# Two extra 512-column products ahead of each head's weight transposes, in the first eight heads of a fused attention and MLP kernel

## The chip, the core and the metric

The kernel runs on one core of a Trainium2 chip. The time is the device time of one execution in microseconds. The core has TensorE (matmuls, PE in the profile, with its weight loads as PEld), VectorE (DVE), ScalarE (ACT), GpSimd (POOL) and SyncE (SP, which issues nearly all DMAs). The engines run side by side, each takes its own instructions in a fixed order, and they wait for each other by semaphores. TensorE's clock is granted at one of two levels, 1.2 and 2.4 GHz; the profile shows it as a share of the higher one.

## What is computed

A causal attention with decay over 4 batches of 8 heads, 576 positions and 64 dimensions, and after it two MLP layers without bias, 512 to 2048 to 512, over the 2304 tokens:

```python
scores = scale * np.matmul(q, k.transpose(0, 1, 3, 2))
cum = np.cumsum(np.log(np.clip(f, 0.0001, 1.0)), axis=-1)
scores = np.where(causal, -1e9, scores + cum[:, :, :, None] - cum[:, :, None, :])
attn = np.exp(scores - np.max(scores, axis=-1, keepdims=True))
attn = attn / (np.sum(attn, axis=-1, keepdims=True) + 1e-09)
x = np.matmul(attn, v)                       # then heads side by side: (2304, 512)
h = x @ w_in;  x = (h - np.tanh(h)) @ w_out  # first layer
h = x @ w2_in; r = np.maximum(h, 0.0); out = (r * r) @ w2_out
```

## The kernel before

The attention is cut into 64 units: 32 for the first 256 queries of every head (`n` below 32) and 32 for the other 320. The first eight units are the eight heads of batch 0. They are worked alone, as two heads at a time, since the first layer can only start when a block of 256 tokens has all its heads; the loop over `astream[:n_start]` near the end of `fused_kernel` does so, with a higher priority (`HOT`). From there on the first layer's products and the other attention units are merged by a table of due times. The order that each engine gets is in the end set by a scheduler: it takes what is ready by its own estimate of times, so that an instruction that is added in one place can change the order around it on all engines.

For a pair of heads TensorE does: four transposes of q and k (`tkq`, line 397, copied to `XF` by VectorE, line 398), the scores (`s`, line 512), the transposes of the softmaxed weights `Pb` (`pt`, in `pt_atom`, lines 539 to 572), copied by ScalarE to `PTF` (line 553), the products with v (`pv`, line 596), scaled by VectorE to `xq` (line 605), and their transposes (`xt`, line 611), which ScalarE and VectorE split into the high and the low part of `x` (lines 663, 664). GpSimd makes the decay (lines 361 and 365), VectorE takes it and the maximum (line 474), and ScalarE the exponential (line 483).

`keep_warm(m)` (line 1000) puts `m` products of 128 by 128 with 512 columns on TensorE. They multiply a tile of ones and write into a bank of PSUM, `warm_out`, that nothing reads (line 1003). Each is held behind what was written on TensorE before it (`keep_in_program_order`); nothing else orders it. Before the change it is called once, ahead of the transposes of unit 0, with `WARM` = 8. The tile `warm` is one of three buffers of a ring `g`, which the first layer's tanh uses later, and `warm_out` is the bank `y1`, which the first layer's sums (`y`, line 819) use later.

The weights come as 64-bit packed words and are decoded while the attention runs: for each of 16 chunks of a layer, `load_w` (line 140) issues two loads of 512 KB, one for either half, on SyncE's queue. `decode_w` takes each half through two conversions on ScalarE (lines 154, 155) and two bit operations on VectorE (lines 161, 163), and then splits each half into a high part (ScalarE, line 176) and a low part (line 177: GpSimd for the first half, VectorE for the second). The first layer multiplies with chunk after chunk: `h` (line 779) needs the chunk's w_in, tanh is taken by ScalarE (line 789), VectorE subtracts it (line 792), ScalarE and VectorE split the difference (796, 800), and `y` (line 819) multiplies it with the chunk's w_out. Every fp32 value is split in two parts of fewer bits so that three fast products replace a slow one. In this text weight 3 is chunk 3 of the first layer, `w_0_3` in the code's names.

Of the kernel before, what the change touches and what calls it, by code (L numbers as in the profile page):

```python
# [18 lines left out]
B, H, S, D = 4, 8, 576, 64  # L19
# [27 lines left out]
WARM = 8  # L47
# [57 lines left out]
def fused_kernel(ctx: ExitStack, tc: tile.TileContext, q, k, v, f, w1i, w1o, w2i, w2o, out):  # L105
# [14 lines left out]
    def bank(tag, n, name):  # L120
        return ps.tile([P, 512], F32, tag=tag, name=name, bufs=n)
# [417 lines left out]
    def pt_atom(i):  # L539

        n, ts = slots[i]
        pb = Pb[i % RING]

        def a():
            while i not in ready_p:
                cw.step()
            if i == 0:
                keep_warm(WARM)
            t = bank("a", 4, f"pt_{i}")
            if len(ts) > 1:  # L550
                for x, (o, c) in enumerate(((0, 0), (128, 0), (128, 1))):
                    nc.tensor.transpose(t[:, x * P : x * P + P], pb[:, o + c * P : o + c * P + P], ident)
                cw.later(LAG['tr'], lambda: nc.scalar.activation(ptf(n), t[:, 0 : 3 * P], AF.Copy))
                return
            if not PT:
                for x in range(2):
                    PT.append(ap.tile([P, 1344], F32R, tag=f"PT{x}", name=f"PT{x}", bufs=1))
                    nc.gpsimd.memset(PT[x][:, 128:192].bitcast(F32), 0.0)
            ti, rows, o, w = ts[0]
            nch = ti + 1  # L560
            for x in range(nch):
                s0 = o + (nch - 1 - x) * P

                nc.tensor.transpose(t[:, x * rows : x * rows + P], pb[:, s0 : s0 + P], ident)  # L564
            src = t[:, 0 : nch * rows].rearrange("p (c r) -> p c r", c=nch)
            dst = [strided(PT[x], *PTC[ti], nch, rows) for x in range(2)]

            def ev():
                nc.scalar.activation(dst[0], src, AF.Copy)  # L569
                cw.later(LAG['trlo'], lambda: nc.vector.tensor_tensor(dst[1], src, dst[0].bitcast(F32), op=ALU.subtract))  # L570
            cw.later(LAG['tr'], ev)
        return 2 * sum((ti + 1) * rows for ti, rows, _, _ in ts), a

    def strided(t, d0, step, m, rows):
        x = t[:, d0 : d0 + rows]
        return bass.AP(tensor=x.tensor, offset=x.offset, ap=[x.ap[0], [step, m], [1, rows]])
# [4 lines left out]
    def ptf(n):  # L581

        return PTF[n % 6 // 3][:, n % 3 * 384 : n % 3 * 384 + 384]
# [416 lines left out]
    def keep_warm(m):  # L1000

        for _ in range(m):
            tc.keep_in_program_order(nc.tensor.matmul(warm_out, lhsT=warm[:, :P], rhs=warm, start=True, stop=True))
# [50 lines left out]
    for s in range(len(steps) + behind):  # L1054
        if s < len(steps):
            i, fc = steps[s]
# [45 lines left out]
```

## Time and profile before

| | |
|---|---|
| Median of 3 runs | 1066.9 us (1065.85 to 1067.23) |
| The profiled execution, its own time | 1066.61 us |
| its span | 1064.9 us |
| mean granted clock | 0.989 |
| TensorE busy | 98% of the span |
| VectorE, ScalarE, GpSimd busy | 56%, 51%, 28% |

A busy share is a mean over stages with different limits. The stages here are: the sums of logs and the first scores (0 to some 20 us), the eight heads (to 41.4 us), block 0 of the first layer merged with further heads while the weights are being decoded (to some 139 us), and then the two layers to the end, with the rest of the attention merged in. Matmuls are pipelined and the profile models their ends, so a product counts as busy for longer than it holds up the next: the distance from one start to the next tells its price. A row of a timeline gives the start, the length, the engine, the line, the operation with what it writes and reads, the count, and in brackets how long the engine stood idle before it and what ended that.

### The profile page before, as it was taken

Reading aid. Unit: us, or ns where it says so; the run is one execution under the profiler, and the core shown is the slowest. Engines: PE = TensorE matmul, PEld = TensorE weight load, DVE = VectorE, ACT = ScalarE, POOL = GpSimd, SP = SyncE. Lnnn points to the kernel's source line nnn. Section 1 sums busy time; section 2 is a strip of 40 time slices with the busy share of each in tenths; the row PEclk is TensorE's granted clock in tenths of the full one; section 3 lists DMA queues with packets and bytes.
Section 4 is the critical chain, followed back from the end, with each engine's and each line's share of the span. In section 5 each row is a group of like instructions: output and inputs, shape, how many; then the busy total and the mean of one; then the engine's idle time right before and its main releaser. Section 6 shows DMA issues by size and latency. Waiting matters only on the chain.

```text
span 1064.9 us, 18194 instructions
## 1 busy us (share of the span) xinstructions
PE 1041.0 (98%) x6545; PEld 934.7 (88%) x6545; DVE 596.3 (56%) x1397; ACT 544.5 (51%) x1179; POOL 293.0 (28%) x468
## 2 busy tenths in 40 slices
PE   7989999999999999999999999999999999999998
PEld 5778899999999999999999887888888888888887
DVE  4897863577777776777854688822322322332332
ACT  5886764566656666666743677622322322222232
POOL 5455532355555555654520121100000000000000
PEclk9998899999999999999999999999999999999999
DMA  8776552242243342433203555300200200010010
GB/s 218 240 214 174 175 150 69 68 125 73 69 128 79 99 118 70 108 98 81 75 21 117 178 189 187 119 1 0 80 1 1 79 1 1 20 40 1 1 40 20
DMA packets 126970, 93.87 MB, mean 88 GB/s; under 512 B 79552, under 2 KB 112128, under 8 KB 126880
## 3 DMA queue, kind: packets, MB, share of 16 engines
q1 hardware_dynamic: 126832, 92.68, 30.1%
q8 instruction: 52, 0.85, 0.3%
q14 instruction: 38, 0.31, 0.1%
q10 hardware_dynamic: 48, 0.03, 0.0%
HBM read 74.26 MB, written 13.71 MB: 83 GB/s over the span
## 4 chain that ended last, share of the span: by engine, by line
PE 79%; DVE 5%; issue 3%; ACT 2%; DMA 1%; POOL 1%; DVEq 0%; ACTq 0%; POOLq 0%
PE h L939 19%; PE o L981 18%; PE h L779 14%; PE y L819 14%; PE pt L564 4%; PE pv L635 3%; PE s L526 2%; PE s L527 2%; DVE wfull L163 2%; PE pv L596 1%; DVE wraw L161 1%; DVE ghl L800 1%; ACT ghl L796 1%; DMA K<-K 1%; POOL w L177 1%
## 5 line engine op out<-in xcount | busy, mean ns | idle before, releaser
L819 PE MATMUL y<-ghl,w 128*128 128x256 f32 (+1 forms) x1536 | 245.2, 303 | 0.1
L819 PEld LDWEIGHTS y<-ghl,w 128*128 128x128 f32 x1536 | 211.3, 192 | 11.7 <-DVE ghl L800 1.9
L779 PE MATMUL h<-x,w 128*128 128x256 f32 x1344 | 205.1, 293 | 9.4 <-POOL w L177 7.5
L939 PE MATMUL h<-y,w 128*128 128x512 f32 (+1 forms) x960 | 209.9, 368 | 0.0
L981 PE MATMUL o<-w,ghl 128*128 128x512 f32 x864 | 209.0, 389 | 0.0
L939 PEld LDWEIGHTS h<-y,w 128*128 128x128 f32 x960 | 169.3, 188 | 31.3
L779 PEld LDWEIGHTS h<-x,w 128*128 128x128 f32 x1344 | 177.1, 192 | 17.2 <-POOL w L177 10.3
L981 PEld LDWEIGHTS o<-w,ghl 128*128 128x128 f32 x864 | 161.1, 188 | 32.7
L952 DVE TENSOR_TENSOR r<-r 128x512 f32<-128x512 f32 (+1 forms) x80 | 51.9, 648 | 216.3 <-ACT r L949 216.3
L949 ACT ACTIVATE r<-h 128x512 f32<-128x512 f32 (+1 forms) x80 | 44.4, 555 | 219.9 <-PE h L939 219.9
L483 ACT ACTIVATE Pb<-Pb,st 128x384 f32<-128x384 f32 (+2 forms) x96 | 67.6, 705 | 69.8 <-DVE st L474 69.7
L369 POOL TENSOR_SCALAR Pb<-neg,ccol 128x384 f32<-128x384 f32 (+2 forms) x96 | 69.2, 721 | 92.2 <-PE pt L564 74.8
L497 POOL TENSOR_SCALAR Pb<-Pb,st 128x384 f32<-128x384 f32 (+2 forms) x96 | 66.0, 688 | 82.5 <-DVE st L493 48.2
L177 POOL TENSOR_TENSOR w<-wfull,w 128x512 fp32r<-128x512 f32 x32 | 43.0, 1342 | 156.9 <-ACT w L176 156.8
L474 DVE CUSTOM_DVE_ANT_0 Pb<-s,Pb 64x288 f32<-64x288 f32 (+2 forms) x160 | 74.0, 476 | 16.4 <-PE s L527 7.7
L957 DVE TENSOR_TENSOR ghl<-r,ghl 128x512 fp32r<-128x512 f32 (+1 forms) x80 | 51.0, 638 | 44.7 <-ACT ghl L953 41.4
L953 ACT ACTIVATE ghl<-r 128x512 fp32r<-128x512 f32 (+1 forms) x80 | 47.1, 588 | 51.5 <-DVE r L952 51.5
L792 DVE TENSOR_TENSOR g<-h,g 128x512 f32<-128x512 f32 x72 | 49.4, 687 | 35.9 <-ACT g L789 34.6
L800 DVE TENSOR_TENSOR ghl<-g,ghl 128x512 fp32r<-128x512 f32 x72 | 55.6, 772 | 23.6 <-ACT ghl L796 23.0
L570 DVE TENSOR_TENSOR PT<-pt,PT 128x384 fp32r<-128x384 f32 (+2 forms) x96 | 55.2, 574 | 10.8 <-ACT PT L569 6.2
L789 ACT ACTIVATE g<-h 128x512 f32<-128x512 f32 x72 | 42.7, 593 | 35.6 <-PE h L779 33.0
L569 ACT ACTIVATE PT<-pt 128x384 fp32r<-128x384 f32 (+2 forms) x96 | 47.9, 499 | 23.4 <-PE pt L564 22.1
(113 smaller groups left out, 1393.5 us busy)
## 6 DMA issues: line engine op xcount, KB each, us to landing
wraw<-in_moe_w_in_dram SPq DMA_DIRECT2D x32, 512.0 KB, 4.2
wraw<-in_moe_w_out_dram SPq DMA_DIRECT2D x32, 512.0 KB, 4.7
neg<-cscr SPq DMA_DIRECT2D x32, 288.0 KB, 3.6
qk<-in_k_dram SPq DMA_DIRECT2D x48, 128.0 KB, 2.6
v<-in_v_dram SPq DMA_DIRECT2D x48, 128.0 KB, 2.6
K<-K SPq DMA_DIRECT2D x32, 144.0 KB, 2.4
yraw<-yscr SPq DMA_DIRECT2D x9, 512.0 KB, 5.0
out_dram<-os SPq DMA_DIRECT2D x16, 256.0 KB, 2.1
```

The costliest lines, as they stand in the source:

```text
L177: (nc.vector if x else nc.gpsimd).tensor_tensor(lo, in0=src, in1=hi.bitcast(F32), op=ALU.subtract)
L369: nc.gpsimd.tensor_scalar(pb[:rows, o : o + w], t[:rows, :w], ccol[:rows, ti, b * H + h : b * H + h + 1], 1.0, op0=ALU.add, op1=ALU.mult)
L474: nc.vector.tensor_tensor_reduce(out=d, in0=t[:rows, src : src + m], in1=d, scale=-0.125, scalar=3.0e38 if j == 0 else stat(0, x)[:rows], ...
L483: nc.scalar.activation(d, d, AF.Exp, bias=stat(len(parts) - 1, x)[:rows], scale=-1.0, accum_out=stat(2, x)[:rows])
L497: nc.gpsimd.tensor_scalar(d, d, r, 1.0, op0=ALU.mult, op1=ALU.mult)
L570: cw.later(LAG['trlo'], lambda: nc.vector.tensor_tensor(dst[1], src, dst[0].bitcast(F32), op=ALU.subtract))
L779: nc.tensor.matmul(o, lhsT=win(0, fc, wh, dc), rhs=xhl[j][:, dc, xh], start=dc == 0 and wh + xh == 0, stop=dc == ND - 1 and wh == 1)
L800: nc.vector.tensor_tensor(ghl[:, 1], g, ghl[:, 0].bitcast(F32), op=ALU.subtract)
L819: nc.tensor.matmul(o, lhsT=wout(0, fc, wh, i * P, P), rhs=ghl[:, xh, fj * n : fj * n + n], start=s == 0 and fj == 0 and wh + xh == 0 and i ...
L939: nc.tensor.matmul(t[:, :n], lhsT=win(1, fc, wh, dc), rhs=yh[i][:, dc, xh, :n], start=dc == 0 and wh + xh == 0, stop=dc == ND - 1 and wh == 1)
L952: nc.vector.tensor_tensor(r[:, :n], r[:, :n], r[:, :n], op=ALU.mult)
L981: nc.tensor.matmul(ob[i][m], lhsT=ghl[:, gh, m * P : (m + 1) * P], rhs=wout(1, fc, wh), start=fc == 0 and gh + wh == 0, stop=fc == NF - 1 ...
```

## The change

In `pt_atom`, `keep_warm` is called for each of the first eight units (H is 8): with 8 as before for unit 0, with 2 for units 1 to 7. That is 14 more products, 22 in place of 8.

```diff
@@ -544,8 +544,8 @@
         def a():
             while i not in ready_p:
                 cw.step()
-            if i == 0:
-                keep_warm(WARM)
+            if n < H:
+                keep_warm(2 if i else WARM)
             t = bank("a", 4, f"pt_{i}")
```

On each engine the same instructions stand as before, apart from the 14 products, and they stand in the same order from shortly after the last weight of the first layer to the end. In between the scheduler orders some of them otherwise. The number behind a name is the number of its unit or chunk (of a block's step for h and y), and the last number only tells buffers apart. First TensorE in the heads, behind the transposes of the first pair's x. Before:

```order
L512 MATMUL s_6_418<-XF1_110 128x256
L611 MATMUL xt_0_371<-ident_87,xq_0_118 128x128 x2
L397 MATMUL tkq_8_411<-ident_87,qk_8_222 128x128
L512 MATMUL s_7_419<-XF1_110 128x128
L512 MATMUL s_7_419<-XF1_110 128x256
```

And now:

```order
L512 MATMUL s_6_424<-XF1_110 128x256
L611 MATMUL xt_0_373<-ident_87,xq_0_118 128x128 x2
L1003 MATMUL warm_117<-warm_115 128x512 x4
L512 MATMUL s_7_425<-XF1_110 128x128
L397 MATMUL tkq_8_417<-ident_87,qk_8_222 128x128
L512 MATMUL s_7_425<-XF1_110 128x256
```

The two products of one unit and the two of the next stand together, four in a row; there are three such rows, and two more products ahead of the transposes of unit 1. Second, VectorE in the first layer's first steps, where weight 3 is decoded. Before:

```order
L177 TENSOR_TENSOR w_0_2_472<-wfull_0_2_408,w_0_2_472 128x512
L161 SCALAR_TENSOR_TENSOR wfull_0_3_606<-wfull_0_3_606 128x512
L163 SCALAR_TENSOR_TENSOR wfull_0_3_606<-wfull_0_3_606 128x512
L161 SCALAR_TENSOR_TENSOR wraw_0_3_386<-wraw_0_3_386 128x512
L398 COPY XF0_109<-tkq_16_801 128x512
L163 SCALAR_TENSOR_TENSOR wfull_0_3_606<-wraw_0_3_386 128x512
L161 SCALAR_TENSOR_TENSOR wfull_0_4_678<-wfull_0_4_678 128x512
```

And now:

```order
L161 SCALAR_TENSOR_TENSOR wraw_0_3_390<-wraw_0_3_390 128x512
L474 ISA Pb3_93,sp2_97<-s_13_674,Pb3_93 128x128
L474 ISA sp2_97 128x1
L163 SCALAR_TENSOR_TENSOR wfull_0_3_620<-wraw_0_3_390 128x512
L474 ISA Pb3_93,sp2_97<-s_13_674,Pb3_93 128x256
L474 ISA sp2_97 128x1
L792 TENSOR_TENSOR g1_0_0_689<-h1_0_0_613,g1_0_0_689 128x512
L605 TENSOR_TENSOR xq_8_122<-pv_8_723,sp0_95 128x256
L177 TENSOR_TENSOR w_0_3_670<-wfull_0_3_620,w_0_3_670 128x512
L161 SCALAR_TENSOR_TENSOR wfull_0_4_692<-wfull_0_4_692 128x512
L163 SCALAR_TENSOR_TENSOR wfull_0_4_692<-wfull_0_4_692 128x512
L398 COPY XF0_109<-tkq_16_815 128x512
```

The copy of tkq_16 stood ahead of weight 3's last bit operation; it now stands behind all of weight 3 and two steps of weight 4. Third, TensorE at the same place. Before:

```order
L779 MATMUL h1_0_1_681<-x_0_114,w_0_2_472 128x256 x12
L611 MATMUL xt_8_740<-ident_87,xq_8_122 128x128 x2
L552 MATMUL pt_10_751<-ident_87,Pb0_90 128x128 x3
L552 MATMUL pt_11_780<-ident_87,Pb1_91 128x128 x3
L397 MATMUL tkq_16_801<-ident_87,qk_16_495 128x128 x4
L512 MATMUL s_14_816<-XF1_110 128x128
L512 MATMUL s_14_816<-XF1_110 128x256
L779 MATMUL h1_0_1_681<-x_0_114,w_0_3_656 128x256 x12
```

And now:

```order
L779 MATMUL h1_0_1_695<-x_0_114,w_0_2_482 128x256 x12
L779 MATMUL h1_0_1_695<-x_0_114,w_0_3_670 128x256 x12
L611 MATMUL xt_8_754<-ident_87,xq_8_122 128x128 x2
L552 MATMUL pt_10_765<-ident_87,Pb0_90 128x128 x3
L552 MATMUL pt_11_794<-ident_87,Pb1_91 128x128 x3
L397 MATMUL tkq_16_815<-ident_87,qk_16_505 128x128 x4
```

The twelve products of h with weight 3 stood behind the transposes of the next heads, and now stand ahead of them. On SyncE one of the two loads of weight 3 moves ahead of the load of v for units 12 to 15.

## Rows read from the trace of the kernel before

**Rows 1.** The page, busy time of each engine:

```profile
PE 1041.0 (98%) x6545; PEld 934.7 (88%) x6545; DVE 596.3 (56%) x1397; ACT 544.5 (51%) x1179; POOL 293.0 (28%) x468
```

**Rows 2.** Stretches: length, busy PE, PEld, DVE, ACT, POOL; granted clock, DMA, GB/s:

```profile
20.50:41.40 20.90, 20.35 (x136) 15.34 (x135) 14.47 (x61) 16.73 (x56) 14.26 (x32) 1.00 0.65 183
...
41.40:60.40 19.00, 14.65 (x87) 12.61 (x86) 17.05 (x35) 15.22 (x34) 5.17 (x5) 0.85 1.01 331
60.40:84.00 23.60, 20.41 (x144) 17.10 (x142) 19.34 (x37) 19.47 (x42) 15.44 (x18) 0.98 0.68 197
84.00:139.00 55.00, 52.05 (x355) 47.09 (x353) 47.13 (x102) 41.08 (x99) 28.77 (x35) 0.88 0.55 159
139.00:1060.00 921.00, 918.50 (x5768) 831.92 (x5769) 488.85 (x1140) 443.01 (x931) 220.81 (x354) 1.00 0.25 71
```

**Rows 3.** Waits of TensorE over the whole span: total, times, longest:

```profile
PE h L779 <- POOL w L177: 7.5, 9, 1.4
```

**Rows 4.** Timeline of TensorE, start and end of the heads:

```profile
16.70 3.48 PE L1003 MATMUL warm<-warm 128*128 128x512 f32 x8
...
21.52 0.66 PE L397 MATMUL tkq<-ident,qk 128*128 128x128 f32 x4 [0.47 <-ACT PTF L553]
...
41.43 1.68 PE L779 MATMUL h<-x,w 128*128 128x256 f32 x12
```

**Rows 5.** The chain that ended last: start, length, what:

```profile
132.97 0.66 PE pt L552 x6
133.62 0.45 PE tkq L397 x4
...
137.59 1.30 POOL w L177
...
901.64 2.72 PE h L939 x12
```

**Rows 6.** Stretches of 2 us, the granted clock third from the end:

```profile
18.00:20.00 2.00, 2.00 (x7) 1.43 (x6) 1.16 (x2) 0.00 (x0) 1.93 (x4) 0.50 0.91 246
...
52.00:54.00 2.00, 2.00 (x11) 1.90 (x9) 0.58 (x1) 2.00 (x5) 0.00 (x0) 0.50 1.09 377
```

**Rows 7.** Timeline of VectorE from the last x to weight 4:

```profile
42.13 0.42 DVE L664 TENSOR_TENSOR x<-xt,x 128x256 fp32r<-128x256 f32 x1
...
47.08 0.28 DVE L474 CUSTOM_DVE_ANT_0 Pb<-s,Pb 128x128 f32<-128x128 f32 x1
...
47.29 0.68 DVE L163 SCALAR_TENSOR_TENSOR wfull<-wraw 128x512 uint32<-128x512 uint32 x1
...
49.73 0.88 DVE L177 TENSOR_TENSOR w<-wfull,w 128x512 fp32r<-128x512 f32 x1
...
54.34 0.69 DVE L398 COPY XF<-tkq 128x512 f32<-128x512 f32 x1 [1.75 <-PE tkq L397]
54.94 0.68 DVE L163 SCALAR_TENSOR_TENSOR wfull<-wraw 128x512 uint32<-128x512 uint32 x1
...
59.27 0.69 DVE L163 SCALAR_TENSOR_TENSOR wfull<-wraw 128x512 uint32<-128x512 uint32 x1
```

**Rows 8.** Timeline of TensorE, tkq_16:

```profile
53.24 1.06 PE L397 MATMUL tkq<-ident,qk 128*128 128x128 f32 x4
```

**Rows 9.** Timeline of GpSimd, weight 3 and weights 4 and 5:

```profile
56.36 1.72 POOL L177 TENSOR_TENSOR w<-wfull,w 128x512 fp32r<-128x512 f32 x1 [6.30 <-ACT w L176]
63.29 3.53 POOL L177 TENSOR_TENSOR w<-wfull,w 128x512 fp32r<-128x512 f32 x2 [5.20 <-ACT w L176]
```

**Rows 10.** Timeline of ScalarE ahead of weight 4:

```profile
60.68 0.60 ACT L789 ACTIVATE g<-h 128x512 f32<-128x512 f32 x1 [0.70 <-PE h L779]
...
62.56 0.65 ACT L176 ACTIVATE w<-wfull 128x512 fp32r<-128x512 f32 x1
```

**Rows 11.** Timeline of SyncE's queue, the load of v:

```profile
40.72 0.92 SPq L304 DMA_DIRECT2D v<-in_v_dram  x2
```

**Rows 12.** DMA issues from 41 to 46 us: count, size, median us to landing:

```profile
wraw<-in_moe_w_out_dram SPq DMA_DIRECT2D x4, 512.0 KB, 8.7
```

## The prediction

> **What bounds the kernel now.** I read the page's busy times first, then the same by stage, then the waits, the timelines of each engine between 40 and 68 us, and last the granted clock. TensorE is busy for 1041.0 of the 1064.9 us [rows 1], so the first thought is that anything added to it lengthens the kernel. The stages say where that holds [rows 2]. From 139 us to 1060 TensorE has 918.50 of 921.00 us: there it sets the end, and what it does before counts only through the moment at which that stretch can begin. From 41.4 to 60.4 us it has 14.65 of 19.00, so 4.35 us stand idle, and from 60.4 to 84 another 3.19. What it waits for there is the decoding of the first layer's weights: nine waits of the h products for GpSimd's last step of a weight, 7.5 us in all up to 139 us [rows 3]. In these 19 us VectorE is the full engine (17.05 us), and it decodes weights too. From 84 to 139 us TensorE is full again (52.05 of 55.00).
>
> The change acts ahead of all this, in the eight heads between 20.5 and 41.4 us. TensorE has 20.35 of 20.90 us there [rows 2] and only one longer wait in its timeline, 0.47 us [rows 4]. So in the heads TensorE is the tight engine, and VectorE (14.47) and ScalarE (16.73) have room.
>
> **The products themselves.** Heads 1 to 7 get two products each, 14 in all. One costs 0.227 us at the full clock (12 products of this shape take 2.72 us [rows 5]), hence 14 x 0.227 = 3.2 us. The eight that are there already cost 3.48 / 8 = 0.435 us each [rows 4], because the clock is granted at 0.50, the 1.2 GHz level, from 18 to 20 us [rows 6]; at that price 14 would be 6.1 us. From 20.5 us to the end of the heads the granted clock is 1.00 [rows 2], the 2.4 GHz level; so I take 3.2, with 6.1 as the upper end. The lower end is near 2.8: two of the 14 now stand in front of a product (tkq) that waited 0.47 us for an evacuation [rows 4] and can hide under that wait. I see no reason for less than that: the products depend on nothing, and the heads show no other such wait.
>
> The Trainium skill ("TensorE: Matmul & The Clock Gate", Back-to-back issue gap) gives a sustained 131 ns for products of 512 columns in a stream with weight loads; by it the 14 would cost an estimated 1.8 us. The trace has 227 ns for such a stream, and the measurement decides.
>
> The products have no semaphore to wait for, and no other engine waits for them. Their bank, y1, is next wanted by the first y products, which come after the first h and its tanh, so holding it longer costs nothing; the same goes for their operand's buffer, whose next user is that tanh. It cannot come earlier, since its own input is made later on the same engine. What is queued behind each pair on TensorE is the rest of its head: the transposes, then the next scores, and at the end the first h product, now at 41.43 us [rows 4]. I put that one at 41.4 + 3.1 = 44.5 us.
>
> **What the delay meets.** Four engines are behind it.
>
> VectorE. The last x of the heads stands at 42.13 us, the last decoding step of weight 2 at 47.29 [rows 7]. In the changed order two of the steps between them (the fourth of weight 1 and the first of weight 2, some 0.6 us each: 0.68 in [rows 7] less the overlap with the next) stand ahead of that x, in the heads, where VectorE has 6.4 us free [rows 2], and a softmax step (0.28 less its overlap, 0.2) stands behind. So weight 2 comes 3.1 - 1.2 - 0.2 = 1.7 us later than now.
>
> Then weight 3. Now its last step stands behind the copy of a product, tkq_16, for which VectorE waits 1.75 us (copy at 54.34, last step at 54.94) [rows 7]; and that product stands on TensorE behind the h of weight 2, at half clock (four tkq products in 1.06 us from 53.24 [rows 8], against 0.45 at full clock [rows 5]). In the changed order all four steps of weight 3 stand ahead of that copy. Weight 2's last step ends at 47.29 + 0.6 + 1.7 = 49.6; from there four steps of 0.6, one of 0.9 on the low part of weight 2 and three softmax steps, some 4.0 us: weight 3 is through at 53.6 where it is now through at 55.5, 1.9 us earlier in spite of the delay. Its GpSimd step, now at 56.36 to 58.08 [rows 9], then frees its h product near 56.
>
> What pays for it: tkq_16 now stands behind the h of weight 3 on TensorE. The h takes some 1.4 us from 56 (twelve in 1.68 us [rows 4]), the twelve transposes 1.3 us at full clock (six pt in 0.66, four tkq in 0.45 [rows 5], two xt): tkq_16 is through at 58.7 instead of 54.3, and VectorE waits about a microsecond for it before the second half of weight 4. Weight 4's last step now begins at 59.27 [rows 7]; by the count it begins between 59.7 and 61.9, depending on the clock in which those transposes run. ScalarE, which splits weight 4 at 62.56, gets there through its own queue [rows 10]: it waits 0.70 us for the h of weight 3, which goes away, and its other work from weight 3 on is the same, which gives some 63.0. I take 1.0 us late at weight 4, of the 3.1 that the heads lost: the rest is in idle time that TensorE had and in VectorE's wait.
>
> SyncE. The loads of weights 3 to 7 are queued behind the load of v, which is issued at 40.72 when the last pair's product has let its buffer go [rows 11]; they move 3.1 us back, but one of weight 3's two halves now goes ahead of v. The second half is issued near 45 and lands, at the 8.7 us that the row has for a crowded queue [rows 12], at 54 in the worst case, or some 4 us earlier if the queue in front of it is as empty as for the first load. ScalarE needs it by 51. This is the term that I know least; it can put up to 2 us on top.
>
> From weight 4 to 139 us the orders differ in a few places only, and each engine waits in turn for the next. I assume the shift is passed on as it is, and put nothing for the few exchanges.
>
> **The sum.** The profiled execution took 1066.6 us (span 1064.9); the median is 1066.9, 0.3 above it. 1066.6 + 1.0 = 1067.6 for such an execution, 1067.9 against the median: +0.1%, which is less than the 0.2% (2.1 us) that a measurement of this kernel can tell from no change. By the terms alone it is from 0.4 us less (the products at 2.8) to 2 us more (weight 3's landing).
>
> **Rivals.** First, slower: TensorE is the bound right through. The heads are full, 84 to 139 us are full, and if weight 4 comes 3 us late the idle time in between is only moved, not used. Then all 3.2 us arrive at the end: 1066.9 + 3.2 = 1070.1. It decides from the point where weight 4 is more than 2.1 us late; the late landing of weight 3 or tkq_16 at half clock does that. For it: each engine takes its work in a fixed order, so a delay at one reaches the others. Against it: 7.5 us of idle time on TensorE between 41.4 and 84 us [rows 2]. Chance 0.31; with the products at half clock it would reach 1073.0, of which I see 0.03 in it.
>
> Second, faster: the earlier weight 3 does more than I count. Now the granted clock is 0.50 from 52 to 54 us [rows 6] and 0.85 as a mean from 41.4 to 60.4 [rows 2], where TensorE waits; if it starts its h later but then waits less, the falls there can go. The twelve transposes with tkq_16 would run in 1.3 us and not twice that, and weight 4 would come some 2.5 us sooner than now, 1.3 from the clock and the rest from weight 3's 1.9: 1066.9 - 2.5 = 1064.4. Chance 0.15. The falls farther back (0.88 as a mean from 84 to 139 us [rows 2]: 13 us at half clock, up to 6.6 us lost) can be moved either way by any shift; that is why the ends of the range are no closer.
>
> Third, the products keep up a clock that would otherwise fall in the heads. In the profile it does not fall there: 1.00 [rows 2]. If it did in the timed runs, each pair's 12 transposes would cost 1.3 us more [rows 5], 5 us for four pairs, and the change would give back about 5 - 3.2 = 2 us: 1065. The three runs of before lie within 1.4 us of each other, which leaves no room for such falls in some of them. Chance 0.02. The Trainium skill (same page, Part 4) says that transposes on TensorE do not count as busy for the clock; by that rule this stretch, full of transposes, would be in danger. The row shows the full clock in it, so the trace does not bear that out here.
>
> **Chances.** Forecast, within 0.2% of before: 0.52. Slower by more: 0.31. Faster by more: 0.17, the second and third rival. The likeliest case alone spans 1065.5 to 1069.0. For 8 in 10 the range takes in the slower rival's 1070.1 with half a microsecond for its clock, and the faster one's 1064.4: 1064.4 to 1070.6.
>
> **What would show it.** The heads: the added products at 0.21 to 0.24 us each with the clock at 1.00 from 21 to 41 us, and the first h product near 44.5 us. The chain: weight 3's GpSimd step some 2 us earlier than 56.36, and weight 4's some 0.5 to 1 us later than 63.29 [rows 9]. TensorE's idle time from the first h to 60.4 us should be well under 4.35. The step fails if weight 3's second half lands after 52 us, if VectorE waits more than 2 us for tkq_16, or if the stretches at half clock after 84 us are more or fewer than the 13 us of now. If the last weight's GpSimd step, now at 137.59 us [rows 5], has moved by about the same as the end, the reading that the end hangs on the decoding is right; if the end moved by 3 us and this step did not, it is wrong.

## The result, and the profile after

The changed kernel takes 1079.2 us (median of four executions, 1075.1 to 1080.7) against 1066.4 for the kernel before beside it: a ratio of 1.0112, with an interval of 1.0096 to 1.0128. That is 12.8 us slower, 11.3 above the forecast and 8.6 above the upper end of its range. The profiled execution has a span of 1078.4 us, 13.5 more than before. Of all executions told of below, one (1087.5 us, of e5) was in a slower state of the chip and stands in no number.

The heads went about as told. Below are TensorE's added products, then the first product of the first layer (before: [rows 4]):

```profile
26.77 1.17 PE L1003 MATMUL warm<-warm 128*128 128x512 f32 x4
...
43.53 2.40 PE L779 MATMUL h<-x,w 128*128 128x256 f32 x18
```

The first layer starts 2.1 us later (41.43 before). GpSimd's steps of weights 3 and 4 (before: [rows 9]) come earlier all the same:

```profile
53.44 1.28 POOL L177 TENSOR_TENSOR w<-wfull,w 128x512 fp32r<-128x512 f32 x1 [3.11 <-ACT w L176]
62.02 1.58 POOL L177 TENSOR_TENSOR w<-wfull,w 128x512 fp32r<-128x512 f32 x1 [7.30 <-ACT w L176]
```

Up to here nothing is lost. The loss begins at a piece of code that the prediction did not name. At slot `SUMS` = 16 the attention calls `more_sums` (line 273), the sums of logs for the second half of the queries. GpSimd first writes a triangle mask `tri1` (line 212) and selects in it (line 213). TensorE multiplies with the mask: `rps` (line 228), which VectorE evicts (line 230), and `cps` (line 238), which VectorE evicts in three pieces (line 240). GpSimd before, from the step of weight 6 to that of weight 8; the mask stands ahead of the decay (lines 361, 365) of units 16 and 17:

```profile
74.28 1.28 POOL L177 TENSOR_TENSOR w<-wfull,w 128x512 fp32r<-128x512 f32 x1 [4.04 <-ACT w L176]
75.50 0.53 POOL L212 MEMSET tri<- 128x512 f32 x1
76.11 0.76 POOL L213 TENSOR_SCALAR_AFFINE_SELECT tri<-tri 128x128 f32<-128x128 f32 x1
76.86 2.62 POOL L361 TENSOR_SCALAR Pb<-neg,ccol 128x128 f32<-128x128 f32 x3
...
81.83 1.26 POOL L177 TENSOR_TENSOR w<-wfull,w 128x512 fp32r<-128x512 f32 x1
88.74 1.27 POOL L177 TENSOR_TENSOR w<-wfull,w 128x512 fp32r<-128x512 f32 x1 [5.65 <-ACT w L176]
```

And after. Weight 6 comes 0.2 us later than before and weight 7 0.6 us earlier (81.22 for 81.83), but the mask now stands behind the decay, 4.6 us later, and weight 8 is 7.6 us late:

```profile
74.51 1.29 POOL L177 TENSOR_TENSOR w<-wfull,w 128x512 fp32r<-128x512 f32 x1 [4.95 <-ACT w L176]
75.78 3.12 POOL L361 TENSOR_SCALAR Pb<-neg,ccol 128x128 f32<-128x128 f32 x3
...
80.12 0.52 POOL L212 MEMSET tri<- 128x512 f32 x1
...
80.95 0.30 POOL L213 TENSOR_SCALAR_AFFINE_SELECT tri<-tri 128x128 f32<-128x128 f32 x1
81.22 1.27 POOL L177 TENSOR_TENSOR w<-wfull,w 128x512 fp32r<-128x512 f32 x1
...
96.34 1.28 POOL L177 TENSOR_TENSOR w<-wfull,w 128x512 fp32r<-128x512 f32 x1 [12.11 <-ACT w L176]
```

TensorE at the sums, before:

```profile
76.76 2.35 PE L228 MATMUL rps<-tri,lfT 128*32 128x320 f32 x10
```

and after:

```profile
80.69 4.40 PE L228 MATMUL rps<-tri,lfT 128*32 128x320 f32 x10 [3.39 <-POOL tri L212]
```

It stands idle for 3.39 us, and then the same ten products take 4.40 us in place of 2.35. The stretch of 20 us from there (length, busy PE, PEld, DVE, ACT, POOL, granted clock, DMA, GB/s) before:

```profile
85.00:105.00 20.00, 19.53 (x137) 18.47 (x137) 16.22 (x39) 13.18 (x32) 10.05 (x12) 0.83 0.49 139
```

and after:

```profile
78.00:80.00 2.00, 0.00 (x0) 0.00 (x0) 1.45 (x3) 1.97 (x5) 2.00 (x3) 0.76 0.70 199
80.00:82.00 2.00, 1.31 (x3) 0.54 (x4) 0.00 (x0) 2.00 (x4) 2.00 (x5) 0.50 1.04 396
...
85.00:105.00 20.00, 20.00 (x98) 18.16 (x98) 11.71 (x28) 7.49 (x18) 2.20 (x3) 0.55 0.28 82
```

From 78 to 80 us TensorE does nothing at all, and in that stretch the granted clock goes from the 2.4 GHz level to 1.2; it stays there for nearly all of the next 20 us, with 98 products done where there were 137. VectorE takes its work in order and shows what that does to the decoding; after:

```profile
85.13 0.48 DVE L230 TENSOR_SCALAR row<-rps 32x320 f32<-32x320 f32 x1 [5.68 <-PE rps L228]
...
91.09 0.19 DVE L240 TENSOR_SCALAR ccol<-cps 128x32 f32<-128x32 f32 x1 [3.74 <-PE cps L238]
...
94.00 0.18 DVE L240 TENSOR_SCALAR ccol<-cps 64x32 f32<-64x32 f32 x1 [1.53 <-PE cps L238]
```

It waits 11.3 us for the sums (with 0.34 for the first cps). Before, it waits 3.4 us, for the second and the third cps alone:

```profile
84.37 0.19 DVE L240 TENSOR_SCALAR ccol<-cps 128x32 f32<-128x32 f32 x1 [2.78 <-PE cps L238]
...
86.40 0.18 DVE L240 TENSOR_SCALAR ccol<-cps 64x32 f32<-64x32 f32 x1 [0.64 <-PE cps L238]
```

In the changed kernel, behind these evictions in VectorE's queue stand the bit operations of weight 8 and the softmax, for which ScalarE waits 6.27 us with weight 8's split right behind:

```profile
95.03 0.40 ACT L483 ACTIVATE Pb<-Pb,sp 128x128 f32<-128x128 f32 x1 [6.27 <-DVE sp L474]
...
95.63 1.15 ACT L176 ACTIVATE w<-wfull 128x512 fp32r<-128x512 f32 x2
```

From there every weight is late; the last one's GpSimd step (137.59 before, [rows 5]) is at 148.57:

```profile
148.57 1.70 POOL L177 TENSOR_TENSOR w<-wfull,w 128x512 fp32r<-128x512 f32 x1
```

That is 11.0 of the 13.5 us. So the theory to be tested (A): the change makes the scheduler put other things in another order; the sums therefore wait for the mask, the clock falls behind that wait, and the decoding is held up. Against it (B): the 14 products cost it by their own time; (C): another exchange in the order does, weight 8's step on GpSimd, which now stands behind two decay steps of unit 18, above all.

### The profile page after: what moved, and what is told of

The parts are those of the page before. It is cut to its first block, busy times and chain, and to the rows that moved or that the text cites. A ratio compares the mean times of both kernels' runs of the same rounds, so it can differ in the third digit from the quotient of the medians.

```text
span 1078.4 us, 18227 instructions
## 1 busy us (share of the span) xinstructions
PE 1050.4 (97%) x6559; PEld 942.7 (87%) x6559; DVE 594.5 (55%) x1397; ACT 544.6 (51%) x1179; POOL 291.6 (27%) x468
## 4 chain that ended last, share of the span: by engine, by line
PE 78%; DVE 5%; issue 2%; ACT 2%; DMA 1%; POOL 1%; DVEq 0%; ACTq 0%; POOLq 0%
PE h L939 18%; PE o L981 18%; PE h L779 14%; PE y L819 14%; PE pt L564 4%; PE pv L635 3%; PE s L526 2%; PE s L527 2%; DVE wfull L163 1%; PE pv L596 1%; DVE ghl L800 1%; DVE wraw L161 1%; POOL w L177 1%; ACT ghl L796 1%; DMA K<-K 1%
## 5 line engine op out<-in xcount | busy, mean ns | idle before, releaser
L819 PE MATMUL y<-ghl,w 128*128 128x256 f32 (+1 forms) x1536 | 248.3, 306 | 0.7 <-DVE ghl L800 0.6
L819 PEld LDWEIGHTS y<-ghl,w 128*128 128x128 f32 x1536 | 214.0, 194 | 12.8 <-DVE ghl L800 2.5
```

What stands on the lines that cost most here:

```text
L819: nc.tensor.matmul(o, lhsT=wout(0, fc, wh, i * P, P), rhs=ghl[:, xh, fj * n : fj * n + n], start=s == 0 and fj == 0 and wh + xh == 0 and i ...
```

## The experiments

In the table, "half clock" is the mean over a kernel's executions of 2 x (1 - mean granted clock) x span, the microseconds at 1.2 GHz; the clock is recorded to three digits, so the column is good to about 1 us. The next columns are of the profiled execution alone: what VectorE waited for the second sums between 74 and 104 us, and the start of the last weight's GpSimd step. That execution is the quickest of its kernel in e11, e12 and e15 and nearly so in e1 and e7.

| kernel | median, us | ratio to before, interval | half clock, us | VectorE's wait | last weight |
|---|---|---|---|---|---|
| before | 1066.4 | 1 | 23.8 | 3.4 | 137.6 |
| changed | 1079.2 | 1.0112 (1.0096 to 1.0128) | 42.0 | 11.3 | 148.6 |
| e1, changed, mask early | 1069.9 | 1.0029 (1.0007 to 1.0050) | 28.2 | 1.4 | 133.3 |
| e2, before, mask late | 1070.3 | 1.0039 (1.0025 to 1.0053) | 27.4 | 8.4 | 143.0 |
| e4, before, mask early | 1070.5 | 1.0043 (1.0025 to 1.0061) | 33.5 | 7.4 | 143.2 |
| e5, changed, 128 columns | 1079.5 | 1.0108 (1.0072 to 1.0143) | 45.2 | 11.3 | 147.3 |
| e13, changed, 2 products | 1077.7 | 1.0100 (1.0062 to 1.0137) | 43.1 | 4.8 | 146.8 |
| e3, changed, fill of 16 | 1062.6 | 0.9970 (0.9955 to 0.9985) | 12.1 | 2.6 | 133.1 |
| e6, changed, 16 elsewhere | 1074.0 | 1.0070 (1.0045 to 1.0096) | 28.3 | 11.3 | 146.0 |
| e7, changed, fill of 10 | 1065.3 | 0.9997 (0.9982 to 1.0011) | 14.5 | 4.3 | 133.5 |
| e9, e7 with 128 columns | 1066.7 | 1.0028 (1.0000 to 1.0055) | 23.9 | 7.4 | 136.3 |
| e11, e3 with 128 in the heads | 1063.2 | 0.9982 (0.9958 to 1.0005) | 22.5 | 2.4 | 130.9 |
| e8, before, fill of 16 | 1058.6 | 0.9934 (0.9913 to 0.9954) | 10.0 | 1.1 | 129.8 |
| e10, e8 with 128 columns | 1061.9 | 0.9961 (0.9945 to 0.9976) | 16.5 | 1.7 | 130.6 |
| e12, before, fill of 8 | 1059.9 | 0.9948 (0.9924 to 0.9972) | 14.8 | 0.9 | 129.3 |
| e14, before, fill of 40 | 1066.9 | 1.0002 (0.9989 to 1.0015) | 18.8 | 3.1 | 135.9 |
| e15, e4 with fill of 8 | 1060.4 | 0.9938 (0.9917 to 0.9959) | 14.8 | 1.0 | 126.9 |

### The mask: e1, e2, e4

e1 and e4 have the same edit, e1 on the changed kernel and e4 on the one before; e2 holds the mask back in the kernel before.

```diff
+                if i == SUMS - 2:
+                    yield 0, make_tri, pvs      # makes tri1
                 if i == SUMS:
                     yield 0, more_sums, pvs     # multiplies with it
```
```diff
-        triangle(tri)
+        tc.keep_in_program_order(nc.gpsimd.memset(tri, 1.0))
+        nc.gpsimd.affine_select(tri[:, 0:P], ...)
```

> The changed kernel, with the second triangle mask (memset L212 and select L213 on GpSimd) asked for two slots earlier, so that it stands on GpSimd ahead of the decay steps of units 14 and 15, some 10 us before the sums need it; the 14 products stay, and so does the new place of weight 8's GpSimd step behind the first decay steps of unit 18. Theory A (the mask comes 4.6 us later, TensorE's sums wait 3.40 us for it, the clock falls to 1.2 GHz for 24 us): no wait of the sums for GpSimd, under 12 us at half clock between 76 and 110 us, the last weight's GpSimd step at 138 to 141 us, the time 1066 to 1071 us. Theory B (the 14 products themselves, by their time on TensorE and the later start they hand on): nothing in that changes, 1076 to 1081 us. Theory C (another exchange of order, weight 8's GpSimd step behind decay steps above all): 1076 to 1081 us as well, with weight 8's step still near 96 us.

> The kernel before, without the added products, with the second triangle mask held behind weight 7's GpSimd step (some 6 us later than it was, 1 to 2 us later even than in the changed kernel). Nothing else is edited. Theory A: TensorE's sums wait 3 to 6 us for the mask, half clock for 20 us or more between 76 and 110 us, the last weight's GpSimd step at 146 to 151 us, the time 1075 to 1081 us. Theory B and C: the mask is nothing that TensorE waits for long, 1065 to 1069 us.

> The kernel before with the mask asked for two slots earlier, as in the first experiment: what that edit does by itself, without the products. In the kernel before the sums had the mask in time (no wait for GpSimd), so theories A, B and C all say 1064 to 1069 us; a gain or loss beyond that would have to be taken off the first experiment's difference.

e1 gives back 9 of the 12.8 us with all 14 products in place, and weight 8's step still behind the decay of unit 18: B and C are far off. Nor is it slower than e4, which has the same edit without the products. But the scheduler also put the sums 7.7 us earlier on TensorE, where they wait for nothing, so e1 does not price the mask alone:

```profile
72.95 2.35 PE L228 MATMUL rps<-tri,lfT 128*32 128x320 f32 x10
```

Its ten executions lie from 1064.1 to 1073.2 us, and the profile is one of the quickest. e2 missed its range: the scheduler also moved the sums behind the h products of weight 7, so that they do not wait for the mask; TensorE waits for weight 7 instead:

```profile
84.33 1.22 PE L781 MATMUL h<-x,w 128*128 128x256 f32 x4 [3.19 <-POOL w L177]
```

e4 was to be neutral and is not. It has no wait for the mask; its sums run from 73.65 us, and so they are no longer there to be worked on while weight 7 is being made:

```profile
82.44 1.01 PE L785 MATMUL h<-x,w 128*128 128x256 f32 x3 [3.36 <-POOL w L177]
...
85.00:105.00 20.00, 19.32 (x109) 17.57 (x109) 12.28 (x28) 9.61 (x24) 6.35 (x8) 0.66 0.20 66
```

Three kernels (the changed one, e2 and e4) have a wait of over 3 us at the same place, one for the mask and two for weight 7. Behind each the clock is low, though in e2 it had fallen already, near 79 us, behind two shorter waits (0.86 and 0.97 us). So A has to be put more widely: not the mask but an idle TensorE near 80 us, whatever it waits for.

### How much of it are the products: e5, e13

```diff
-                keep_warm(2 if i else WARM)
+                keep_warm(*((2, 128) if i else (WARM,)))   # e5: 128 columns
```
```diff
-            if n < H:
+            if n == 0 or 1 <= n < 2:                       # e13: one head
```

> The changed kernel with its 14 added products cut from 512 to 128 columns. Every engine's instructions stand in the very order of the changed kernel; only the products' own time falls, from 14 x 0.23 = 3.2 us to about a quarter of it. Theory A (what costs is the order, which makes TensorE wait some 3 us near 80 us, and the clock that falls behind that wait): the wait of the sums for the mask is still there (2.5 to 4.5 us), half clock for 20 us or more between 76 and 125 us, the time 1074 to 1081 us. Theory B (the products' own time and the later start they hand on): the loss goes with the columns, 1066 to 1070 us.

> The changed kernel with 2 of its 14 products left, those of the second head; the third to eighth head have none. The scheduler's order is again another: GpSimd writes the mask straight behind weight 6 but selects it only behind four decay steps, and TensorE's order ahead of the sums is nearly that of the changed kernel. Theory A (order, then wait, then clock): the sums wait 2 us or more for the mask's select, half clock for 10 us or more between 76 and 125 us, 1070 to 1081 us. Theory B (each product costs its share): 2/14 of 12.8 us, 1067 to 1069 us.

In e5 every instruction stands where it does in the changed kernel. Four products of 128 columns take 0.64 us in place of 1.17 (about a half, not the quarter expected), the wait and the fall are the same, and so is the time. The interval is wide: it leaves room for a microsecond or two from the columns, but not for the 1066 to 1070 us of B:

```profile
26.98 0.64 PE L1003 MATMUL warm<-warm 128*128 128x128 f32 x4
...
80.21 4.40 PE L228 MATMUL rps<-tri,lfT 128*32 128x320 f32 x10 [3.39 <-POOL tri L212]
```

In e13 two products are left, and 1.0% is still lost, but most of it at another place. Weight 6's step comes 5.2 us later than before (79.53 for 74.28). From 62 to 70 us the granted clock is 0.50, and VectorE waits for a product with v (line 596) that stands behind 22 y and 12 h products; the bit operations of weight 6 stand behind that wait:

```profile
DVE xq L605 <- PE pv L596: 4.5, 1, 4.5
```
```profile
79.53 1.28 POOL L177 TENSOR_TENSOR w<-wfull,w 128x512 fp32r<-128x512 f32 x1 [8.10 <-ACT w L176]
```

Then the sums are cut in two by the mask's select, which the scheduler put behind most of the decay of units 16 and 17:

```profile
82.00 1.26 PE L228 MATMUL rps<-tri,lfT 128*32 128x320 f32 x4
85.50 1.28 PE L228 MATMUL rps<-tri,lfT 128*32 128x320 f32 x6 [2.24 <-POOL tri L213]
```

Behind them the clock is as in the kernel before (0.83 from 85 to 105 us); it has 0.81 to 0.89 in each stretch of 20 us from 45 to 145 us. So e13 says nothing of the mask's wait, but much on B: a seventh of the products lose as much as all, by another exchange and another fall.

### Filling the wait: e3, e6, e7, e9

```diff
     def more_sums():
         ...
         triangle(tri)
+        keep_warm(16)          # e3; e7: 10; e9: 10 of 128 columns
         sum_logs(1, tri, row[: B * H])
```
```diff
+                if i == SUMS - 5:
+                    yield 0, (lambda: keep_warm(16)), pvs     # e6
```

> The changed kernel with 16 more products of 512 columns that nothing reads, put on TensorE straight ahead of the second sums, so that it works through the 3.4 us in which it waited for the mask. The mask is as late as in the changed kernel. Theory A1 (what costs is the clock that falls behind the wait): the sums start at 80 to 82 us as in the changed kernel, at the full clock; half clock under 10 us between 76 and 110 us; the time 1067 to 1072 us. Theory A2 (what costs is the wait itself, handed on): the same lateness, 1077 to 1083 us.

> The changed kernel with 16 more products of 512 columns, as in the third experiment, but put among the first products of the MLP some 20 us ahead of the sums, where they fill no wait for the mask. The order of the engines stays that of the changed kernel but for a few neighbours. Theory A: the sums still wait 2 to 4 us for the mask, the clock falls for 15 us or more between 76 and 125 us, the time 1073 to 1084 us. Rival D (16 products anywhere keep the clock up and gain what the third experiment gained): 1061 to 1066 us.

> The changed kernel with 10 products of 512 columns ahead of the second sums in place of the 16 of the third experiment: 2.3 us of work for a wait of 3.4 us, with GpSimd in the very order of the changed kernel (weight 8's step behind the first decay steps of unit 18 too). Theory A: about 1 to 2 us of wait are left, the clock does not fall for long (under 10 us of half clock between 76 and 110 us), the time 1061 to 1068 us. Theory C (weight 8's place on GpSimd costs the time): 1075 to 1081 us. If the clock falls in spite of the fill, 1070 to 1078 us.

> The seventh experiment's kernel with its 10 filling products cut from 512 to 128 columns. Every engine's instructions stand in the very order of the seventh experiment's kernel; only some 1 us of the fill goes (four products of 128 columns took 0.64 us in the fifth experiment, four of 512 columns 1.17 us), so that the sums should wait 3.2 to 3.6 us for the mask where they waited 2.40 us. Theory A1 (a wait of some 3 us drops the clock): half clock for 10 us or more between 76 and 125 us, the time 1068 to 1077 us. Theory O (what the fill gained is its order, with products of the second matrix kept back for the wait): no change from the seventh, 1063 to 1068 us.

More products that nothing reads, put at the right place, turn the loss into a gain. In e3 the mask is as late as in the changed kernel, but TensorE has been at work until 1.80 us before it, and the sums run at the full clock:

```profile
74.36 3.83 PE L1004 MATMUL warm<-warm 128*128 128x512 f32 x16
...
81.74 2.35 PE L228 MATMUL rps<-tri,lfT 128*32 128x320 f32 x10 [1.80 <-POOL tri L212]
...
85.00:105.00 20.00, 18.57 (x160) 17.16 (x159) 19.14 (x44) 16.00 (x39) 10.83 (x12) 1.00 0.70 208
```

e3 proves less than it seems, since the 16 products also move the order: the scheduler keeps y products back for the wait. Its time is 4 us under what A1 expected for it. e7 has GpSimd's order unchanged, weight 8's place with it, and its time is that of the kernel before: C has fallen.

```profile
81.14 2.35 PE L228 MATMUL rps<-tri,lfT 128*32 128x320 f32 x10 [2.40 <-POOL tri L212]
```

e9 has e7's order on every engine and a microsecond less of fill. In its profile the sums waited 4.60 us, not the 3.2 to 3.6 expected, and ran at half clock:

```profile
82.39 4.40 PE L228 MATMUL rps<-tri,lfT 128*32 128x320 f32 x10 [4.60 <-POOL tri L212]
...
85.00:105.00 20.00, 20.00 (x156) 17.32 (x155) 15.69 (x35) 11.87 (x27) 7.33 (x10) 0.95 0.48 135
```

Its ten executions fall in two groups: six from 1063.6 to 1067.1 us, at mean clocks of 0.990 to 0.994, and four from 1070.6 to 1074.8, at 0.982 to 0.986. The median, 1066.7, lies below what A1 expected (1068 to 1077) and fits Theory O; the upper group is in A1's range. The profile is of the lower group: a longer wait than the changed kernel's and the same slow sums, but the clock is at 1.00 again from 88 us on, and the time is near that of the kernel before. So the wait alone does not make the loss; in the changed kernel the clock also stays low behind it, from 80 to 102 us at 0.50. The mean span of e9 is 3.3 us above e7's (1066.95 for 1063.65): in this one order, that is what the shorter fill costs. What makes the upper group 7 us slower than the lower one no trace shows.

e6 is the control: its 16 products came to stand at 44.4 us, 35 ahead of the sums and not the 20 expected. They leave the wait and the fall where they were:

```profile
79.01 4.40 PE L228 MATMUL rps<-tri,lfT 128*32 128x320 f32 x10 [3.38 <-POOL tri L212]
```

It is 5 us quicker than the changed kernel. Its granted clock from 45 to 65 us is 1.00, 0.84 in the changed kernel, and its sums come 1.7 us earlier; whether these two make the 5 us is not shown.

### Without the products of the heads: e8, e10, e12, e14, e15, and e11

The same edit in the kernel before (`keep_warm` with 16, 16 of 128 columns, 8 and 40), in e15 on e4; e11 cuts the heads' products of e3 to 128 columns.

> The kernel before with 16 products of 512 columns ahead of the second sums, none in the heads. If theory A holds, the 14 products of the heads cost what the head alone can show once the clock stays up: the third experiment less this one, forecast as +1.0 us. This kernel then stands at 1060 to 1064 us, with no half clock between 70 and 110 us. Theory B: the third experiment's kernel carries the products' whole loss, and this one is 10 us or more below it, 1048 to 1053 us.

> The eighth experiment's kernel (no products in the heads) with its 16 filling products cut from 512 to 128 columns, every engine's order unchanged: 1.6 us less of work ahead of the second sums, whose wait for the mask grows from 0.47 to about 2 us. Theory A1: a wait of 2 us was survived in the third and seventh experiments (1.80 and 2.40 us), so the clock stays up and the time stays at 1057 to 1061 us; if the clock falls here, 1062 to 1070 us. Theory O: 1057 to 1061 us.

> The eighth experiment's kernel with 8 filling products of 512 columns in place of 16, in search of the cheapest fill (the order around the sums differs a little). Theory A1: as long as no wait of 3 us is left near 80 us the clock stays up, and the time is 1057 to 1061 us, at best 1.9 us below the eighth; with such a wait and the clock fallen, 1064 to 1072 us.

> The fourth experiment's kernel (no products in the heads, mask asked for two slots earlier, 1070.5 us) with 8 filling products of 512 columns ahead of the second sums. If the fourth lost its 4 us to the 3.36 us that TensorE waited for weight 7 behind its early sums, and the clock that fell there, the fill and the products that the planner keeps back with it end that: no wait of 2 us for weight 7, no half clock between 76 and 110 us, 1057 to 1061 us. If the early mask itself cost the fourth its time: 1068 to 1072 us.

> The third experiment's kernel with the 14 products of the heads cut from 512 to 128 columns, every engine's order unchanged: what the columns themselves cost where the clock stays up. They take 14 x (1.17 - 0.64) / 4 = 1.9 us less of TensorE in the heads. Theory A with the prediction's path (the head's shift is passed on in part): 0.3 to 1.9 us below the third experiment, 1060.5 to 1062.5 us. Theory B: the 4.0 us that the third lies above the eighth are the columns' time, and half of them goes: 1060 to 1061 us. If nothing changes, the 4.0 us are the order's.

> The eighth experiment's kernel with 40 filling products of 512 columns in place of 16: the second sums come some 24 x 0.235 = 5.6 us later on TensorE, with the engine at work all the time, so that lateness stands without a fall of the clock. Theory V (what a late sum costs is VectorE, which waits for it in its queue with the weights' decoding behind it): VectorE waits 4 to 7 us for the sums, the time 3 to 7 us above the eighth, 1062 to 1066 us. Theory A1 in its strict form (only the clock costs): no half clock between 76 and 125 us, 1058 to 1061 us.

e8 is 0.7% quicker than the kernel before and 1.9% quicker than the changed one (1058.6 to 1079.2), though it has 16 useless products; that is 1.4 us under what was expected of it. e12 and e15 stand within its interval: there is no best size to be told from these runs. e15 came where it was told if the wait for weight 7, and not the early mask, had cost e4 its time; the fill moves the order as well. In the profiled execution, the quickest of its four, the clock does not fall at all in the 80 us that decide (first line e15, second the changed kernel):

```profile
76.00:156.00 80.00, 77.36 (x627) 71.82 (x627) 63.59 (x149) 58.94 (x145) 42.93 (x56) 1.00 0.58 173
```
```profile
76.00:156.00 80.00, 69.87 (x426) 61.03 (x427) 54.09 (x120) 50.76 (x121) 34.49 (x48) 0.77 0.47 140
```

e10, in e8's order with 1.9 us less of fill, is 3.2 us slower, between the two answers that were set down for it. In its profile the clock does fall in a wait of 2.05 us for the mask, though not for long (0.50 from 76 to 78 us, 1.00 from 80 us on):

```profile
75.73 1.27 PE L228 MATMUL rps<-tri,lfT 128*32 128x320 f32 x2 [2.05 <-POOL tri L212]
```

e3 and e8 differ by 4.0 us, with nearly the same half clock. e11, in e3's order, takes half of the columns' time out of its heads and measures the same within the intervals. But the two are not alike in clock: three of e11's ten executions, near 1069 us, have a mean clock of 0.985, and its half clock is 22.5 us for e3's 12.1. By the rate worked out below that is an estimated 3.3 us, so half of the columns may be worth some 1.6 us. In e3 the mask also comes at 81 us and in e8 at 75. How the 4.0 us divide between the columns and the later mask stays open, and what the 14 products would cost with nothing reordered no run here shows.

e14 was to make VectorE wait for late sums at the full clock, and did not. The sums came late (from 82.24 us), but VectorE had other work until 90.82 us; TensorE waited 3.26 us for its eviction of the first cps, and the clock fell there.

```profile
91.44 1.92 PE L238 MATMUL cps<-lfT,tri 128*128 128x32 f32 x8 [3.26 <-DVE ccol L240]
...
85.00:105.00 20.00, 16.74 (x107) 14.51 (x106) 14.37 (x33) 13.39 (x29) 6.18 (x8) 0.74 0.46 139
```

Its time, 8 us above e8, is above what either theory told, and it separates nothing.

### The share of the clock

The executions themselves give another measure. Within one kernel the order is fixed, and the executions still differ. Taken as differences from their kernel's mean, 209 executions of 17 kernels (87 of them of the kernel before) show 0.32 us more of span for each microsecond more at half clock, with a correlation of 0.84. By that rate the 18.2 us more of half clock in the changed kernel (42.0 for 23.8) make 5.8 of the 12.3 us by which the mean spans differ; 6.5 stay for the waits and the other order. e6 fits: the changed kernel's order with 13.7 us less of half clock, which makes 4.4 us, and it is 4.9 quicker in the mean span. So does e9 against e7: 9.4 us more of half clock, which makes 3.0 of the 3.3. The split is an estimate: a longer wait brings both a fall and a delay, and no run here has one without the other.

## Why the prediction was wrong

**The products.** Right. Forty of them in a row took 9.24 us (e14), 0.231 each, for the 0.227 used, and the heads ran at the full clock (0.99 as a mean from 20.5 to 43.5 us). The 131 ns of the Trainium skill ("TensorE: Matmul & The Clock Gate", Back-to-back issue gap) are not borne out for them.

**The first h product.** Told for 44.5, it came at 43.53: of the 3.2 us about one was hidden in the heads. Weight 3's GpSimd step was told some 2 us earlier than 56.36 and came 2.9 earlier. Its second half can't have been late for that. TensorE's idle time from the first h product to 60.4 us, told to be well under 4.35, is 4.35 again (12.52 of 16.87 us busy).

**Weight 4.** Told 0.5 to 1 us late, it came 1.3 early, although VectorE waited 2.57 us for tkq_16, more than the bound that was set for this step. By weight 7, at 81 us, the kernel was 0.6 us ahead. The shift of 1.0 us that the sum carries through did not arrive.

**The step that failed** is the sentence on the rest: "I assume the shift is passed on as it is, and put nothing for the few exchanges." One of these exchanges was the mask behind the decay steps, and there the loss begins. It could be priced beforehand: the decay steps that went ahead of the mask take 4.3 us on GpSimd (2.62 + 1.15 + 0.48 in the trace of before), and in the kernel before the mask was written only 0.7 us ahead of the first product that needs it (75.50 + 0.53 = 76.03; first product at 76.76). So a wait of some 3 us, 3.39 as measured, was to be read from the order and the trace; what it would do to the clock, only runs could tell. The prediction did say that the falls after 84 us can be moved either way, at up to 6.6 us, and gave them half a microsecond at the upper end of its range. From 84 to 139 us the granted clock is 0.73 as a mean: 29 us at half clock in place of 13, which the prediction's last paragraph named as a sign of failure.

What is shown is that the order and not the products' time makes the loss (e5 in the same order, e1, e13). That the loss goes through TensorE's wait near 80 us, the low clock behind it and VectorE's wait is read from the trace, and agrees with the fills (e3, e7) and with the control (e6). Open are the shares of these three, and why the clock came back so late.

**The rivals.** The slower one (TensorE the bound right through, 1070.1) had the sign but not the mechanism or the size: e5 and e13 lose as much with half or a seventh of the products' time. Of the faster one the first half came true (weight 3 earlier, weight 4 too), and was overtaken at 78 us. The third played no part.

**The reading of the end** was right: it hangs on the last weight. That step moved by 11.0 us and the end by 13.5; the other 2.5 come behind it. In the profiles of the table the span less this step's start is 927 to 932 us.

## What to carry to other kernels

Where a scheduler orders the engines, an edit's own cost may be the smallest part of it: list every exchange in the order, on the engines that the edit does not touch too, and price each by who waits for the moved instruction and what stands behind that waiter. Look first at places where a short producer feeds a tight engine with no slack, and at TensorE idle for some microseconds while other engines wait for it in order. Work that nothing reads can pay there, if it stands in that very wait; 35 us ahead of it, the wait stayed.

## What was not expected of the hardware

In seven profiles TensorE stood idle for 3.19 to 4.60 us at a stretch between 75 and 92 us, waiting for the mask, for weight 7 or for VectorE (the changed kernel, e2, e4, e5, e6, e9, e14). In six of them the clock went to 1.2 GHz within that stretch or right behind it; in e2 it was there already, after two waits of 0.9 us. In e3, e7 and e11 (1.80 to 2.40 us) the clock was 1.00 from 78 to 105 us. But the length of one wait does not decide it: in e10 it fell in a wait of 2.05 us, and in the kernel before from 85 to 92 us behind one of 1.45. The Trainium skill ("TensorE: Matmul & The Clock Gate", HAM oscillation) tells of the same pattern with waits for DMAs: TensorE goes cold in the wait, and the next products run at the lower clock. The 4.40 us of the sums after 3.39 us of idleness, against 2.35, agree.

What was new is how long it stays low, and how unevenly: the mean from 85 to 105 us is 0.55 in the changed kernel, 0.64 in e5 with the same order, and 0.95 in e9. TensorE counted as busy for all 20 us in each of the three. e9 had y products left to work on behind the sums; whether that is why its clock came back sooner was not tried.

The same program on the same chip then takes times up to 11 us apart (e9), in step with its mean clock. A change of the order moves not just one time but the odds of several.
